# Re-searched queue orders and engine choices in a one-core four-layer linear-attention kernel

## The chip, the cores and the metric

One Trainium2 chip (trn2), one core of it. The metric is the device time of one execution in microseconds (us), taken as the median of several runs. Most runs lie within 0.5 us of their kernel's median, so the comparisons below use several rounds in which both kernels run on the same chip. All runs named here are of the undisturbed ("fast") state, with a granted TensorE clock of 0.999 or 1.000 (one run of b_head2, its slowest, has 0.996). The profiler's span of a run is about 2.1 us shorter than its device time (377.4 against 379.55 us for the run of the kernel before that was profiled).

Engines are called by the profile's names: PE (TensorE, matmuls), PEld (its weight loads), DVE (VectorE), ACT (ScalarE), POOL (GpSimd), SP (SyncE, here only the queue that issues transfers). An eviction is an operation of ACT or DVE that copies a matmul result out of PSUM (the tiles `ps`, which all 2519 matmuls of the trace of before write) to SBUF, where the program keeps the other operands. A transfer lands when its last part has arrived.

## The reference

Sequence 2048, width 512, 32 heads of 16, hidden width 1376, bf16. Two kinds of layer in turn, four in all:

```python
x = x + attn(layernorm(x));  x = x + glu(layernorm(x))     # layers L0/A0 and L1/B1
x = x + attn(layernorm(x));  x = x + glu(layernorm(x))     # layers L2/A2 and L3/B3

def attn(x):                                  # linear attention
    q, k, v = split_heads(x @ wqkv)
    phi = lambda z: concat(softmax(z @ w_phi), softmax(-(z @ w_phi)))   # per head, 16 -> 32
    kv, z = phi(k)^T v, sum_s phi(k)
    return (phi(q) kv) / (phi(q) z + 1e-6) @ wo
def glu(x):
    g = x @ W_gate
    return (g * (g > 0) * (x @ W_up)) @ W_down
```

In the kernel a row tile has 128 rows, so there are 16 tiles. "Key scaling" is the division of the exponentials of a key tile by their sums (phik), "query scaling" the same for queries (phiq), "numerator" is phi(q) kv (num). Before phi(q) can be multiplied it is transposed by a DMA transfer (qtr); there are 143 such 128 KB transposes in all.

## The kernel before

The program is a list of 3963 operations, each with an engine, what it reads and writes, and a name. Two tables decide how it runs: `ORDER` gives each engine's queue, as operation numbers in base 36, and `CHOICE` names the operations whose engine differs from the default. Waits are semaphores worked out from the tables.

```python
ORDER = {"act": ("29 26 6 25 ..."), "dve": (...), "pool": (...), "pe": (...), "sp": (...)}   # cut
for _e, _n in (("pool", ("kvf zero;...")), ("dve", (...)), ("act", (...))):                 # cut
    ...
            CHOICE[_x] = _e

def schedule(self):
    self._derive_deps()
    ops, TO = self.ops, self.TO
    seq = {e: [int(x, 36) for x in ORDER[e].split()] for e in ENG_NAMES}
    assert sorted(i for s in seq.values() for i in s) == list(range(len(ops)))
    ...                                                                                     # cut
```

The softmax here doesn't subtract the row's maximum and nothing guards it: scores larger than these inputs give would overflow.

Of the kernel before, what the change touches and what calls it, by code (L numbers as in the profile page):

```python
# [14 lines left out]
        "29 26 6 25 27 28 2a 2b 4t 2c 39 49 3u 4y 4e 44 5i 5n 58 5s 4j 6j 6k 67 73 72 8l 6d 84 6a 4o 83 8k 91 9x 9y 7r 96 9z c4 c5 9b c6 9g d9 da db b4 f9 f8 "  # L15
        "fm fl ay ee ef b2 eg gz gy fz h0 hx hw fy ij g5 g4 ik gb ga gg gh ii hv mk mj n4 n3 mu mt lm lq lt ne nd nn no nt r8 o5 o4 rf of op oq jv kn p0 pa pb "
        "vg pl pw pv vk q6 qg qh qr s1 ko sd sc sn xw xt sx sy t8 lg tt tj ti zn u4 ue u3 zu up uo uz wd wo wp x9 wz xa m8 ru ym yn xk z7 11o z8 yx 10k 11s zi "
        "10l 11v 10v 142 w2 12t yb 149 146 134 13p 135 13f 109 159 14z 13q 15a 15u 12a 15v 15k 14o 16x 178 177 17i 1b7 16m 18l 1aw 1c9 1db 1ad 1by 1d0 1e6 1dv "
        "1ea 1f0 1fg 1ew 1em 1gj 1fw 1gk 1fc 1gi 1jm 1hk 1hl 1hj 1kb 1fs 1ib 1ic 1kr 1l7 1g8 1ia 1j2 1j3 1gx 1ll 1lk 1j1 1m9 1ma 1nv 1k6 1ob 1mz 1my 1lj 1or "
        "1l3 1kn 1p7 1nn 1m8 1mn 1no 1mx 1pl 1pk 1ly 1q9 1nm 1o7 1nc 1qa 1pj 1qz 1qy 1on 1rq 1rp 1q8 1s4 1p3 1qx 1s3 1py 1ro 1t5 1t6 1s5 1s6 1t8 1qn 1t7 1u7 "  # L20
        "1ua 1u8 1xr 1uw 1uv 1u9 1xx 1y3 1uy 1ym 1yn 1ux 1z1 1z2 1y9 1yl 1zh 1zg 1z0 1zv 1zw 1zf 24t 1zu 24u 255 24v 24w 256 258 230 257 25u 25t 25h 25i 25k "
        "25w 25v 25j 26q 271 27d 272 22j 27n 27c 27z 27o 27y 289 28a 28l 28k 28v 28w 297 29h 296 29i 29t 29s 2be 23c 23x 2bp 2bq 24i 2cc 2cb 2c1 26f 2c0 2dj "
        "2cn 2cm 2di 2dt 2b3 2e5 2du 2e4 2ef 2eg 2er 2eq 2ft 2fu 2hu 2i5 2i6 2ih 2ig 2j2 2ir 2j3 2a7 2is 2d7 2kg 2k6 2kh 2k5 2l2 2l3 2ks 2kr 2mh 2le 2mg 2ld "
        "2fi 2hb 2ju 2m5 2qa 2pz 2qb 2n8 2ql 2qw 2qx 2qm 2sa 2r7 2sl 2sb 2r8 2ny 2sw 2sx 2t7 2sm 2pg 2t8 2um 2tj 2ti 2ul 2g8 2rz 2mv 2ua 2vw 2x5 2ak 2v0 2xg "
        "2xr 2xh 2od 2y3 2xs 2y2 2vd 2yd 2yp 2ye 2yo 2z0 2zb 2yz 2zm 2za 2zl 2gl 2wo 2zw 2zx 308 2wb 307 30z 2oq 31c 30m 322 "),
    "dve": (
        "2z 30 33 3a 3b 3e 3l 3m 3v 3k 3w 3p 2m 53 3z 5d 5x 5z 5t 5v 5u 60 5y 5w 7i 7g 7f 7h 6l 64 6m ao 74 ap 75 an am 85 7t 86 8m a0 7x 8n 7v a3 a1 a4 c7 ca "
        "c8 cb dc df b0 fa dg fn dd fo fb eh ek el ei em h1 h2 fq h4 hy hz h5 i1 il im i0 in io j2 j1 j3 j4 ix jd iz je iy j0 k6 jj k7 ku ky l1 l2 jo l3 l4 jp "
        "l6 l7 lv lw ju kc ly lz nu kh rc rg ki rh og ld ri o6 le or p1 rk pc pm rl vn vo q7 m5 px vq qi m6 xp qs kp s2 vs so se r4 sz xy xz t9 rr tk tu y1 u5 "
        "uf uq zr 13s we lh v0 zw zx zy zz rs vc 13t vz x0 wq w0 y8 y9 xb yo xl 13v 106 107 17w yy 15x zj 15y m9 z9 17x 15z 10m 17y 1b9 1ba 19o 10w 12u 11y 181 "  # L30
        "19p 14c 120 121 136 118 14d 13g 16c 14e 16d 150 19r 1cb 127 11k 13r 15b w3 128 1cc 18b 18c 15w 15l 1cd 14l 14m 16y 16j 16k 17j 179 17v 18i 18j 1a3 1a4 "
        "1bo 1bp 19b 1cq 1cr 18z 1aa 1ab 1b8 1dl 1ax 1dm 19n 1bv 1cx 1bw 1cy 1ca 1e8 1ds 1dt 1e7 1eb 1dc 1ey 1fe 1f3 1fh 1d1 1en 1ex 1jk 1kp 1fu 1fx 1gl 1fj "
        "1ft 12b 1k9 1fd 1l8 1ks 1gy 1dw 1hm 1g9 1hn 1j4 1j5 1gm 1id 1ha 1go 1nt 1l5 1nw 1mb 1ie 1i1 1hp 1mc 1la 1o9 1is 1k7 1jj 1p5 1oc 1gn 1os 1op 1ko 1p8 "
        "1lm 1ln 1n0 1ig 1n1 1n2 1l4 1lo 1pm 1lz 1lp 1nd 1np 1mo 1j7 1nq 1pn 1po 1r0 1pp 1r1 1o8 1r3 1qb 1qc 1s7 1s8 1oo 1p4 1rr 1rs 1se 1sf 1pz 1qo 1t9 1tg "
        "1rf 1xp 1ta 1th 1qe 201 1xs 1sw 1xv 202 203 20f 1xu 1ty 1tl 204 20g 1y1 208 209 1yo 1um 1y7 1y6 1yp 1z3 1ya 1yq 1z4 1yc 1zi 1zj 1zl 1zx 1zy 200 1zz "
        "20a 21r 21q 21s 21p 20d 221 222 227 22u 22v 22c 23n 23o 22d 20m 22i 248 249 235 236 265 23b 20n 2et 26r 266 2gm 2eu 24f 23u 23v 273 2ev 27e 2gn 280 "
        "28b 27p 2at 24g 2au 28m 2go 2lg 298 2cx 29j 28x 29u 2cy 2j5 26c 2j6 26d 2n9 2na 2f8 2f9 2bf 23d 2a6 2lh 2br 2aj 2li 2ll 2b0 2h1 2cd 2c2 2h2 2d4 2ff "
        "2co 23y 2b1 2or 2os 2dk 2nc 2d5 2fg 2e6 2eh 2dv 2es 2tl 2fv 2jk 2jl 2g7 2ra 2ou 2b4 2hv 2rb 2i7 2ow 2lv 2tm 2lw 2gk 2it 2h8 2h9 2ii 2j4 2no 2m2 2k7 "
        "2np 2rf 2m3 2jr 2js 2l4 2ki 2kt 2p6 2p7 2lf 2mi 2mu 2rp 2nv 2nw 2rq 2n7 2m6 2u0 2u1 2qc 2q0 2hc 2jv 2op 2oc 2vm 2pd 2qn 2qy 2pe 2r9 2sc 2rw 2rx 2vn "
        "2t9 2sn 2sy 2tk 2un 2uz 2u7 2u8 2vt 2vu 2vc 2x6 2xt 2ub 2xi 2wa 2yf 2wn 2y4 2yq 2s0 2zn 2z1 2zy 2zc 309 30l 30y 31b 31o 320 "),  # L40
    "pool": (
        "2p 0 1 4 2t 5 2w 2x 31 2 2u 2n 2o 32 3c 34 3d 3n 3o 2y 3x 3y 3f 2s 2r 2q 2v 61 62 66 63 69 6c 3 7j 7l 7k 7m 7n 7o 6n 7p 7q 76 ar aq as au at 87 av aw "
        "ax 8o a2 a5 c9 cc dh fp fc de fd ff ej h3 fs en h6 l5 lu lx rj jw vp jx vr vt xx kq y0 zv y2 100 13u 13x 17z li 11w rv 160 11x 14a 14b ma 162 19q 1bb "
        "1be 11z 10a yc 19t 14f 1bc yd 1cg rw w4 1ce 10b 18m 14p 1ec 16n 1ed 1f1 1f2 1fi 1fy 1fz 1jn 1kc 1kd 1bz 18n 16o 1ke 14q 1jo 1kt 1jp 1c0 1ku 1l9 1ae "
        "1ho 12c 1nx 1p9 1dx 1pa 1if 1od 1md 1ny 1oe 1ot 1j6 1d2 1ou 1me 1n3 1af 1r2 1nr 1ns 1sg 1sj 1s9 1sc 1rt 1qd 1sa 1tb 1te 1tc 1xt 206 1sh 1ti 1tj 20h "
        "1y4 1y5 20k 1xy 1xz 1y0 1ru 1yr 1yb 1z6 1z5 1zk 20i 20b 20o 20r 20p 2ew 2gr 2gp 22k 22l 2ey 2j7 2j8 23e 26g 2ja 24j 2nb 24k 23z 2lj 2ot 2b5 2tn 2to "
        "2tq 2d8 26h 2ne 2rc 2rd 2d9 2hd 2fj 2fk 2nz 2o0 2jw 2vx 2ph 2m7 2s1 2pi 2uc 2vy "),
    "pe": (
        "7 8 9 a b c d e f g h i j k 4p 4q 4r 4s l m n o p q r s t u v w x y z 35 36 37 38 10 11 12 13 14 15 16 17 3g 3h 3i 3j 18 45 46 47 48 3q 3r 3s 3t 4z 50 "
        "51 52 59 5a 5b 5c 4u 4v 4w 4x 4a 4b 4c 4d 40 41 42 43 5e 5f 5g 5h 4f 4g 4h 4i 5j 5k 5l 5m 19 1a 1b 54 55 56 57 1c 1d 1e 5o 5p 5q 5r 1f 1g 6f 6g 6h 6i "  # L50
        "1h 6y 6z 70 71 1i 1j 1k 1l 1m 1n 1o 8g 8h 8i 8j 1p 1q 1r 1s 6p 1t 1u 7z 80 81 82 1v 1w 6o 1x 1y 1z 20 21 22 23 24 4k 4l 4m 4n 9l 9m 9n 9o 8x 8y 8z 90 "
        "9h 9i 9j 9k 9p 9q 9r 9s 9t 9u 9v 9w 6q 6r 6s 6t 77 78 79 7a 92 93 94 95 bo bp bq br bs bt bu bv 6u 6v 6w 6x 97 98 99 9a 88 89 8a 8b bw bx by bz c0 c1 "
        "c2 c3 ct cu cv cw 9c 9d 9e 9f cx cy cz d0 d1 d2 d3 d4 d5 d6 d7 d8 f4 f5 f6 f7 fh fi fj fk 7b 7c 7d 7e 8c 8d 8e 8f 8p 8q 8r 8s dy dz e0 e1 a6 a7 a8 a9 "
        "e6 e7 e8 e9 e2 e3 e4 e5 ea eb ec ed fu fv fw fx ae af ag ah cd ce cf cg cl cm cn co 8t 8u 8v 8w aa ab ac ad gm gn go gp gi gj gk gl ai aj ak al ch ci "
        "cj ck gq gr gs gt gu gv gw gx di dj dk dl g0 g1 g2 g3 hn ho hp hq dq dr ds dt ia ib ic id cp cq cr cs dm dn do dp hr hs ht hu g6 g7 g8 g9 du dv dw dx "
        "es et eu ev eo ep eq er gc gd ge gf ie if ig ih mb mc md me mf mg mh mi f0 f1 f2 f3 ew ex ey ez h7 h8 h9 ha hf hg hh hi i2 i3 i4 i5 ip iq ir is hb hc "
        "hd he hj hk hl hm i6 i7 i8 i9 it iu iv iw j5 j6 j7 j8 j9 ja jb jc mz n0 n1 n2 mv mw mx my k2 k3 k4 k5 jf jg jh ji jy jz k0 k1 ml mm mn mo mp mq mr ms "
# [55 lines left out]
    "sp": (  # L113
        "2d 2e 2g 2f 2h 2i 2j 2k 2l 68 65 6e 6b 7u 7s 7y 7w b5 b1 az bg b3 bi bm b7 bn bb fg fe bk b9 ft fr bc ba b6 bd b8 be bj bf bh l8 bl m0 nv lf rm m7 s3 "
        "vu y3 101 w1 ya rt 108 13w wf 13y 161 122 12v 163 182 16e 14g 180 1bd 19s 18d 14n 1cf 19u 1bf 16l 129 18k 1ch 1a5 1bq 1cs 1dn 1ac 1bx 1e9 1cz 1du 1ez "
        "1ff 1kq 1ay 1fv 1jl 1ka 1l6 1k8 1p6 1nu 1oa 1oq 1xq 1sk 1tf 1xw 1y2 1sb 1sd 1y8 1tk 1tm 1si 207 205 1td 20c 20e 20l 23p 20j 24a 20s 267 26s 23w 20q "
        "24h 2av 2ex 2gq 2gs 2ez 2cz 2bg 2fa 2lm 2jb 26e 2fh 2d6 2b2 2h3 2j9 2lk 2ox 2jm 2lx 2hw 2nd 2nf 2ov 2nq 2ha 2m4 2jt 2tr 2p8 2re 2rg 2nx 2rr 2tp 2pf "
        "2q1 2vo 2u2 2ry 2u9 2vv 2x7 321 "),
}
# [257 lines left out]
CHOICE = {}  # L377
# [836 lines left out]
```

## Time and profile before

| | kernel before |
|---|---|
| device time, median of the first 3 runs | 379.65 us (379.38 to 380.29) |
| profiled span | 377.4 us |
| busy PE / DVE / ACT / POOL | 367.7 / 276.2 / 227.0 / 130.8 us |
| idle time of PE between its first and last matmul (worked out in the prediction) | about 8.7 us |

The prediction shows the page, the chain, the waits and the windows of this kernel. The view of the timeline: start in us, busy time in us, engine, line of the kernel, operation, output and inputs with their shapes, how many; a bracket gives the idle time before it and what ended it. First, the root of tile 3 on POOL (9.43), the scaling of tile 3 on DVE (10.33), and what POOL runs beside it:

```profile
9.43 0.86 POOL L631 TENSOR_TENSOR rstd<-rv,mhalf 128x1 f32<-128x1 f32 x1
...
10.33 0.41 DVE L670 TENSOR_SCALAR ytile<-x_sb,mv,rstd 128x512 bf16<-128x512 bf16 x1
10.38 0.40 POOL L668 TENSOR_SCALAR nrx<-rstd 128x1 f32<-128x1 f32 x1
10.55 1.89 POOL L568 MEMSET vsb<- 128x128 bf16 x3
```

DVE starts 0.05 us before POOL's next operation.

### The profile page before, as it was taken

What the parts mean: (1) busy time and instruction counts of PE and PEld (TensorE: products, weight loads), DVE (VectorE), ACT (ScalarE), POOL (GpSimd) and SP (SyncE); (2) the same over time, 40 slices, a digit from 0 to 9 for tenths busy, and PEclk for the clock granted to TensorE, in tenths of its full rate; (3) what the DMA queues carried; (4) which work ended last, traced back from release to release, by engine and by line L of the source; (5) the groups of instructions that cost most, each with busy time, mean ns of one, the idle gap of its engine ahead of it and who ended that gap; (6) DMA issues with size and microseconds to landing.
All of it is one profiled execution on the core that took longest, in us unless ns stands there. A gap on an engine that the chain in (4) does not pass through costs nothing.

```text
span 377.4 us, 6882 instructions
## 1 busy us (share of the span) xinstructions
PE 367.7 (97%) x2519; PEld 203.9 (54%) x2565; DVE 276.2 (73%) x607; ACT 227.0 (60%) x463; POOL 130.8 (35%) x234
## 2 busy tenths in 40 slices
PE   6999999999999999999999999999999999999997
PEld 5654555877744454454444446577664454445443
DVE  5999998989968676459799999898984654342323
ACT  3999878765744127874677568584635451653450
POOL 6799941133344001350463577023221201000020
PEclk9999999999999999999999999999999999999999
DMA  7632794313326444310300045335543442142012
GB/s 233 173 76 52 187 240 149 77 33 56 78 43 94 97 64 84 70 30 14 70 2 1 2 81 95 79 63 95 83 83 75 81 86 56 28 71 70 30 42 70
DMA packets 87856, 29.33 MB, mean 78 GB/s; under 512 B 79792, under 2 KB 86800, under 8 KB 87824
## 3 DMA queue, kind: packets, MB, share of 16 engines
q1 hardware_dynamic: 84368, 25.86, 33.7%
q10 hardware_dynamic: 3456, 3.05, 2.5%
q8 instruction: 20, 0.33, 0.4%
q14 instruction: 12, 0.10, 0.1%
HBM read 7.91 MB, written 2.10 MB: 27 GB/s over the span
## 4 chain that ended last, share of the span: by engine, by line
PE 85%; POOL 7%; DVE 3%; issue 2%; ACT 1%; DMA 1%; POOLq 0%; DVEq 0%
PE ps L962 37%; PE ps L1011 20%; PE ps L725 7%; PE ps L942 7%; POOL expk L750 5%; PE ps L822 5%; PE ps L988 3%; PE ps L921 2%; PE ps L787 1%; PE ps L886 1%; DMA hT<-in_A_wqkv_dram 1%; DVE Zk L744 1%; POOL rstd L648 1%; PE ps L868 1%; PE ps L539 0%
## 5 line engine op out<-in xcount | busy, mean ns | idle before, releaser
L962 PE MATMUL ps<-yT,Wgu 128*128 128x512 bf16 (+2 forms) x870 | 150.8, 320 | 0.6
L962 PEld LDWEIGHTS ps<-yT,Wgu 128*128 128x128 bf16 x880 | 78.5, 98 | 58.8 <-ACT expk L970 1.0
L964 ACT ACTIVATE gate_sb<-ps 128x512 bf16<-128x512 f32 (+2 forms) x110 | 50.7, 480 | 55.1 <-PE ps L962 41.8
L1011 PE MATMUL ps<-Wd,hT 128*128 128x512 bf16 (+4 forms) x354 | 79.3, 373 | 0.5
L1011 PEld LDWEIGHTS ps<-Wd,hT 128*128 128x128 bf16 (+1 forms) x363 | 34.6, 98 | 39.5 <-DVE hT L972 0.7
L972 DVE TENSOR_TENSOR hT<-gate_sb,expk 128x512 bf16<-128x512 bf16 (+2 forms) x70 | 23.9, 361 | 30.4 <-ACT expk L970 21.4
L970 ACT ACTIVATE expk<-ps 128x512 bf16<-128x512 f32 (+2 forms) x70 | 32.0, 475 | 22.2 <-PE ps L962 19.5
L710 ACT ACTIVATE sq<-x_sb,nmr 128x512 bf16<-128x512 bf16 x48 | 34.6, 721 | 10.3 <-DVE x_sb L687 6.6
L744 DVE TENSOR_REDUCE Zk<-expk 128x64 f32<-128x1024 bf16 x32 | 38.1, 1203 | 1.0 <-ACT expk L737 0.7
L714 POOL TENSOR_TENSOR rstd<-rv,mone 128x1 f32<-128x1 f32 x32 | 18.6, 589 | 50.2 <-DVE rv L712 50.0
L1013 DVE SCALAR_TENSOR_TENSOR x_sb<-ps,rstd,x_sb 128x512 bf16<-128x512 f32 (+2 forms) x33 | 23.9, 728 | 16.1 <-PE ps L1011 13.5
L942 PE MATMUL ps<-wo_p,oT 128*128 128x512 bf16 x118 | 30.8, 379 | 0.6 <-DVE oT L413 0.3
L975 DVE TENSOR_TENSOR hT<-gate_sb,ps 128x512 bf16<-128x512 bf16 (+2 forms) x40 | 21.7, 544 | 12.6 <-ACT gate_sb L964 6.4
L855 POOL TENSOR_TENSOR expq<-expq,rho 128x256 bf16<-128x256 bf16 x36 | 22.2, 624 | 24.4 <-DVE rho L852 23.7
L847 DVE TENSOR_REDUCE Zq<-expq 128x64 f32<-128x1024 bf16 x24 | 28.8, 1204 | 0.8 <-POOL rho L852 0.5
L687 DVE SCALAR_TENSOR_TENSOR x_sb<-ps,x_sb 128x512 bf16<-128x512 f32 x32 | 21.9, 687 | 8.6 <-PE ps L942 7.8
L750 POOL TENSOR_TENSOR expk<-expk,rZk 128x1024 bf16<-128x1024 bf16 x13 | 25.9, 2005 | 0.6 <-DVE rZk L746 0.6
L755 POOL TENSOR_TENSOR expk<-expk,rZk 128x512 bf16<-128x512 bf16 x17 | 19.1, 1134 | 11.8 <-DVE rZk L746 11.5
L822 PE MATMUL ps<-Wqp,yT 128*128 128x512 bf16 x91 | 22.8, 379 | 0.3
L725 PE MATMUL ps<-Wkp,yT 128*128 128x512 bf16 x84 | 22.0, 379 | 0.2
L725 PE MATMUL ps<-wv_p,yT 128*128 128x512 bf16 x85 | 21.9, 379 | 0.2
L712 POOL TENSOR_SCALAR rv<-rv 128x1 f32<-128x1 f32 x22 | 4.3, 203 | 45.3 <-ACT sq L710 45.3
(126 smaller groups left out, 514.1 us busy)
## 6 DMA issues: line engine op xcount, KB each, us to landing
out_dram<-x_sb ACTq DMA_DIRECT2D x15, 128.0 KB, 1.7
x_sb<-in_A_x_dram SPq DMA_DIRECT2D x3, 512.0 KB, 5.0
Wgu<-in_B_W_up_dram SPq DMA_DIRECT2D x4, 344.0 KB, 5.5
Wgu<-in_B_W_gate_dram SPq DMA_DIRECT2D x4, 344.0 KB, 4.3
Wd<-in_B_W_down_dram SPq DMA_DIRECT2D x5, 256.0 KB, 3.3
yT<-ytile SPq DMA_TRANSPOSE x56, 2.5
qT<-expq SPq DMA_TRANSPOSE x40, 2.5
x_sb<-in_A_x_dram SPq DMA_DIRECT2D x4, 128.0 KB, 3.6
```

The lines of the kernel that those rows point to most:

```text
L710: op("act", lambda e: e.activation(k.sq[:], k.x_sb[:, t, :], ACT.Square, scale=-float(D), bias=k.nmr[:, t, :], accum_out=k.rv1[:, t, :]), ...
L725: op("pe", (lambda ic, bank, W: lambda e: e.matmul(k.pb[bank][:], k.yT[:, ic, t * 128:(t + 1) * 128], W[:, ic, :], start=(ic == 0), stop=( ...
L744: op("dve", lambda e: e.tensor_reduce(k.Zk[:, zb, :], k.expk[:, t, :, :, :].rearrange("p g s (h f) -> p (g s h) f", f=16), AX.X, ALU.add), ...
L750: op("pool", lambda e: e.tensor_tensor(kv, kv, k.rZk[:, rb, :].unsqueeze(2).to_broadcast([P, 64, 16]), ALU.mult), [r("expk", t, 0), r("exp ...
L822: op("pe", (lambda ic, bank, tt: lambda e: e.matmul(k.pb[bank][:], k.yT[:, ic, tt * 128:(tt + 1) * 128], k.Wqp[:, ic, :], start=(ic == 0), ...
L847: op("dve", lambda e: e.tensor_reduce(k.Zq[:, b, :], k.expq[:, t, :, :, :].rearrange("p g s (h f) -> p (g s h) f", f=16), AX.X, ALU.add), ...
L942: op("pe", (lambda c, bank: lambda e: e.matmul(k.pb[bank][:], k.oT[:, ob, c, :], k.wo_p[:, c, :], start=(c == 0), stop=(c == NC - 1)))(c, ...
L962: op("pe", (lambda bank, W, ic, fc, Mf: lambda e: e.matmul(k.pb[bank][0:Mf, 0:n], W[:, ic, fc * 128:fc * 128 + Mf], k.yT[:, ic, c0:c0 + n] ...
L964: op("act", (lambda Mf, gb, gs: lambda e: e.activation(k.gate_sb[0:Mf, gs, 0:n], k.pb[gb][0:Mf, 0:n], ACT.Relu))(Mf, gb, gs), [self.RP[gb] ...
L970: op("act", (lambda Mf, ub, up: lambda e: e.activation(up[0:Mf, 0:n], k.pb[ub][0:Mf, 0:n], ACT.Copy))(Mf, ub, up), [self.RP[ub]], ru, 170 ...
L972: op("dve", (lambda Mf, up, gs, u: lambda e: e.tensor_tensor(k.hT[0:Mf, u, 0:n], k.gate_sb[0:Mf, gs, 0:n], up[0:Mf, 0:n], ALU.mult))(Mf, u ...
L1011: op("pe", (lambda fc, Kf, u, c0, bank, m0, m1: lambda e: e.matmul(k.pb[bank][:, m0:m1], k.hT[0:Kf, u, c0:c0 + 128], k.Wd[0:Kf, fc, m0:m1] ...
```

## The change

A scheduler searched the orders and engines once more. The issues of the initial loads keep their order; the early layer-norm scalings may now take POOL (none does); the table load is modelled as 250 instead of 1450 ns, which is a number for the scheduler only. No arithmetic, tile or transfer is added or removed. The new tables put 106 operations on another engine (56 from POOL to DVE, 40 from DVE to POOL, 5 each way between ACT and DVE) and reorder the rest.

```diff
 ORDER = {
     "act": (
-        "29 26 6 25 27 28 2a 2b 4t 2c 39 49 3u 4y ...          # all five queues replaced, cut
+        "29 26 6 25 27 28 2a 2b 39 2c 3k 49 5d 4y ...
@@ CHOICE: the three lists of names replaced, cut
-        op("act", lambda e: e.activation(k.sq[:, 0:1], ones_c[:, 0:1], ACT.Exp), ..., 1450, "table")
+        op("act", lambda e: e.activation(k.sq[:, 0:1], ones_c[:, 0:1], ACT.Exp), ..., 250, "table")
-            self.op2("act" if on_act else "dve", apply, dep, dst, {"dve": 407, "act": 825}, f"{tag} apply {t}", 250.0)
+            how = CHOICE.get(f"{tag} apply {t}", "act" if on_act else "dve")
+            other = "act" if how == "dve" else "pool" if t < 9 and how == "act" else "dve" if how == "act" else "act"
+            dd = {"dve": 407, "act": 825, "pool": 2090}
+            self.op2(how, apply, dep, dst, {e: dd[e] for e in (how, other)}, f"{tag} apply {t}", 250.0)
```

The numbers of `ORDER` say nothing to a reader. These are three stretches of it, with the operations' names:

```text
POOL, start      before: rv1 3 | rstd 3 | nrx 1 | v ones 3 | v ones 2 | v ones 1 | h10t zero | rv1 4
                 after:  nrx 1 | rv1 3 | rstd 3 | mask4 | h10t zero | v ones 2 | rv1 4
POOL, 224-235 us before: phiq 6 1 | ... | phik 11 1 | phik 12 1 | rx 15 | phik 13 1 | phik 13 0 | phik 14 0 | phiq 6 0 | phiq 5 0
                 after:  phiq 3 1 | ... | phiq 6 0 | ... | phik 11 1 | rx 15 | phik 13 0 | phik 12 1 | phik 13 1 | phik 14 0
SP, 228-244 us   before: qtr 3 0 | qtr 3 1 | qtr 1 0 | qtr 4 1 | qtr 4 0 | qtr 2 0 | qtr 5 0 | qtr 5 1 | qtr 6 1 | otr 2
                 after:  qtr 3 0 | qtr 6 0 | qtr 4 0 | qtr 5 1 | qtr 4 1 | qtr 3 1 | otr 2
```

## The prediction

> **What bounds the kernel now.** I read the page's busy shares first, then the chain that ended last in order of time, then the waits of the weight loads, then the windows by stage. The first view says which engine is full.
>
> ```profile
> span 377.4 us, 6882 instructions
> ...
> PE 367.7 (97%) x2519; PEld 203.9 (54%) x2565; DVE 276.2 (73%) x607; ACT 227.0 (60%) x463; POOL 130.8 (35%) x234
> ...
> PE 85%; POOL 7%; DVE 3%; issue 2%; ACT 1%; DMA 1%; POOLq 0%; DVEq 0%
> ```
>
> PE is busy nearly always and carries 85% of the chain. Busy PE is not PE at its peak, so I need its floor. The chain in order of time gives the pace of each matmul width, since there matmuls stand back to back:
>
> ```profile
> 9.72 0.45 PE ps L585 x8
> 120.13 5.18 PE ps L962 x24
> 133.95 0.99 PE ps L988 x12
> 227.60 0.76 PE ps L787 x24
> 248.84 2.18 PE ps L962 x20
> ...
> 370.68 3.70 PE ps L1011 x19
> ```
>
> So 128 columns take 56 ns, 512 take 216, 192 take 82.5, 68 take 32, 256 take 109; the 144-wide ones stand at about 63 (0.25 us for 4). Counts from the loops of the code: 1333 of 512 columns (128 each of v, k, q, wo; 480 gate/up; 341 down) make 287.9 us; 240 of 256: 26.2; 11 of 384 at some 162: 1.8; 128 of 192: 10.6; 64 of 144: 4.0; 267 of 128: 15.0; 448 of 68: 14.3; four small ones 0.4. That is 360.2 us of real matmuls. Another 70 are dummies that multiply ones by ones: 3.9 us. Sum 364.1. The first matmul starts at 1.6 us, the last ends at 374.4; the 3.0 us after it are residual and store. So 374.4 - 1.6 - 364.1 = about **8.7 us is all the idle time PE has**. Where it lies is in the waits of the weight loads, taken stretch by stretch (0 to 14 us, 50 to 68, 230 to 252, 252 to the end):
>
> ```profile
> PEld ps L539 <- POOL ones L527: 1.6, 1, 1.6
> PEld ps L678 <- DVE ytile L670: 1.4, 1, 1.4
> PEld ps L585 <- DMA hT<-in_A_wqkv_dram: 0.8, 1, 0.8
> ...
> PEld ps L921 <- issue: 0.8, 2, 0.5
> PEld ps L886 <- DVE expk L413: 0.7, 1, 0.7
> ...
> PEld ps L942 <- DVE oT L413: 0.4, 1, 0.4
> ...
> PEld ps L962 <- ACT expk L970: 1.0, 3, 0.3
> PEld ps L1011 <- DVE hT L972: 0.7, 2, 0.4
> ```
>
> Added up, these views give 4.5 us before 14 us (1.6 of it the lead-in already taken off), 1.1 from 14 to 50, 2.1 from 50 to 68, 1.9 from 68 to 230, 1.8 from 230 to 252, 2.1 after. They over-count a little (11.9 against 8.7), as each counts a weight load's normal spacing too. The windows show which other engines are full meanwhile:
>
> ```profile
> 14.00:53.00 39.00, 38.68 (x306) 20.52 (x311) 38.51 (x55) 37.35 (x57) 35.76 (x42) 1.00 0.54 108
> 53.00:66.00 13.00, 11.81 (x98) 6.61 (x96) 11.16 (x30) 8.99 (x13) 1.50 (x3) 1.00 0.58 201
> 66.00:120.00 54.00, 53.58 (x468) 36.39 (x476) 47.24 (x125) 32.43 (x95) 16.28 (x34) 1.00 0.33 63
> 120.00:230.00 110.00, 109.36 (x593) 52.42 (x604) 85.14 (x173) 67.28 (x131) 42.34 (x76) 1.00 0.26 49
> ```
>
> From 14 to 53 us PE, DVE, ACT and POOL are all at 92% or more: nobody can take work from anybody. From 66 us on PE alone is full, with the clock at 1.00.
>
> [...] 624 against 468 ns for the 128x256 scaling, 1152 against 428 ns for the 128x512 sum; and only operations between SBUF tiles trade places with POOL in the diff, PSUM evictions only between ACT and DVE.
>
> **The change part by part.** No matmul, tile, transfer or arithmetic is added or removed. Of 3963 operations 106 change engine; the rest are reordered within their queues.
>
> *Layer-norm scaling on GpSimd.* The code now lets the early scalings take POOL, but comparing the engine lists none of them does. Worth 0. Likewise the new 250 ns for the table load is only a number for the scheduler.
>
> *Engine moves.* POOL to DVE, 56: 17 query scalings (468 ns on DVE, 624 on POOL, from the rows by form), 4 key scalings (827, 1134), 2 sums (428, 1152), 5 denominators' products (222, 335), 1 (268, 445), 7 ratios (179, 308), 13 variance fixes (145, 203), 7 negations (140, 274). DVE gains 17.6 us, POOL loses 26.3. DVE to POOL, 40: 6 query and 5 key scalings, 2 sums, 6 small products (2, 3 and 1 of three kinds; the second 184, 272), 5 ratios, 12 variance fixes, 4 negations: DVE loses 12.3, POOL gains 18.8. ACT and DVE swap ten PSUM evictions, DVE +0.35, ACT nearly 0. Net: DVE 276.2 + 5.7 = **about 282**, POOL 130.8 - 7.5 = **about 123**. All of it lies beside PE. By the time at which these operations stood before, DVE gets some 1.7 us more between 60 and 100 us, 1.1 from 100 to 120 and 1.3 from 240 to 260, almost nothing before 60.
>
> *Start, 0 to 14 us.* Five more dummies (43 instead of 38) run before the fourth transpose of the key weights, in time that waits for input anyway; so five fewer stand later: 5 x 56 = 0.28 us at best. The copy of transposed tile 1 goes to ACT and that of weight block 0 to DVE. The second weight transpose stands ahead of tile 2's, which takes 4 x 56 = 0.22 us off what follows the arrival of tile 2, so the second v eviction on ACT could go at some 11.1 us instead of 11.29. These overlap; I take -0.3 us. More is not to be had: the inputs' issues are fixed, and tile 2 arrives when it arrives.
>
> *14 to 53 us.* Same work on four full engines, the POOL chain of key scalings (1.93 us each) in the same order: the 0.2 us carries through, nothing adds.
>
> *53 to 66 us.* I compared the queues: key/value mask, first denominators, num 0, q 11, q 10, num 1, output transpose, the two last feature-major q groups, num 2 stand in the same order on PE, with two pairs swapped that wait for the same eviction. The 2.1 us of waits stay. 0.
>
> *66 us to the end.* PE has about 5 us of small waits by the over-counting view, some 3.5 in truth. At 230 to 252 the order (num 0, q 10, q 9, otr 0, num 1, wo 0, num 2) is the same, so 1.2 us of these stay. Of the remaining 2.3 a new search may save a few tenths and a fuller DVE may cost a few: -0.1.
>
> Sum: -0.3 + 0 + 0 - 0.1 = -0.4 us: **379.2 us**.
>
> **The rivals.** First, the search finds real gains in the small waits: half of the late 2.3, plus 0.5 at the start, plus some of 50 to 68 us: -2.2, so 377.4. For it: the waits are of 0.2 to 0.7 us, which order alone could fix. Against: the orders around the largest are unchanged. Second, DVE becomes the bound from 60 to 120 us, where it has only about 7 us of idle time and gets 2.8 more; PE has PSUM banks to free there. Each late eviction would cost 0.2 to 0.4 us; a handful makes +1.5, so 381. For it: 47.2 of 54 us is an average and some slices are full. Against: the moved operations are mostly off the eviction path. Third, the late weights: the DMA share from 50 to 60 us is 1.02, and the order of the 18 weight loads and of the query transposes among them changes. If an output-projection block or the last gate block lands late, PE waits at 60 or 66 us: +1, so 380.6. Against: before, DMA falls to 0.08 at 60 us, 5 us ahead of the first gate matmul, and the new order puts the projection blocks earlier.
>
> **Range and chances.** The rivals sit at -2.2 and +1.5; runs of one kernel spread over 0.9 us. 377.7 to 380.9 should hold 8 in 10. Faster by 2% needs 7.6 us out of 8.7 us of idle time, half of it before the inputs land: 1 in 100. Slower by 2% needs a broken stage: 2 in 100. Within 2%: 97 in 100.
>
> **What would show it.** PE busy should be within 1 us of 367.7; DVE 280 to 284 and POOL 121 to 126 show the engine moves. The key scaling chain on POOL should start 0.1 to 0.3 us earlier than 18.46 us. The 0.7 us wait on the feature-major numerator's eviction and the 0.4 us on the output transpose's copy should still be there. I am wrong if waits of the weight loads from 66 us on fall below 2 us or exceed 8, if the first gate matmul waits for DMA, or if the stage before 53 us moves by more than 0.5 us.

The sum came to -0.4 us, so 379.2 us. The 216 ns for 512 columns in the count rest on the 24 matmuls in 5.18 us of the chain shown; that no pace can be lower, which would make 364 us a floor, is not shown. The 0.2 to 0.4 us for a late eviction are an estimate; single waits of weight loads for evictions late in the trace of before are as long (0.2 for `ACT vsb`, 0.3 for `ACT expk`, 0.4 for `DVE oT`).

## More of the kernel before

A fill is a memset.

The operations that the argument touches. The layer-norm scaling of tiles 2 and 3 of the first layer ("L0 apply") waits for POOL's reciprocal root ("L0 rstd") and feeds PE's transposes:

```python
op("pool", lambda e: e.tensor_tensor(k.rstd[:, t0:t1, :], k.rv1[:, t0:t1, :], k.mhalf[:, 0:n], ALU.pow), ...)   # "L0 rstd t"
op("dve", lambda e: e.tensor_scalar(k.ytile[:, yb, :], k.x_sb[:, t, :], k.mv[:, t, 0:1], k.rstd[:, t, :],
                                    op0=ALU.subtract, op1=ALU.mult), ...)                                       # "L0 apply t"
```

Fills on POOL that may run at any time before their first use:

```python
for st in range(NSLAB):
    op("pool", ... e.memset(k.vsb[:, st*4:st*4+4, :, 16:17], 1.0) ...)          # "v ones st"
op("pool", lambda e: e.memset(k.h10t[:], 0.0), ...)                             # "h10t zero"
op("pool", lambda e: e.tensor_tensor(k.mask4[:], k.mask8[:, 0:4], k.mask8[:, 4:8], ALU.add), ...)   # "mask4"
op("pool", lambda e: e.tensor_copy(k.kvf[:, :, 136:144], ...), ...)             # "kv ones"
```

Key scaling in two halves u, by choice on DVE or POOL; query scaling and the two transposes of a query tile:

```python
self.op2(..., e.tensor_tensor(kv, kv, k.rZk[...].to_broadcast([P, 32, 16]), ALU.mult), ...)     # "A2 phik t u"
for u in range(2):
    self.op2("pool", ... e.tensor_tensor(ev, ev, k.rho[...].to_broadcast([P, 4, 4, 16]), ALU.mult) ...)   # "A2 phiq t u"
    self.dma_tr(... e.dma_start_transpose(qb[:, u*4:u*4+4, :], k.expq[:, t, u*4:u*4+4, :, :]...) ...)     # "A2 qtr t u", SP
```

Second, near the end of the keys of the last attention, POOL's key scalings 13 0 and 14 0 (in one group) and DVE's 14 1:

```profile
231.39 2.69 POOL L755 TENSOR_TENSOR expk<-expk,rZk 128x512 bf16<-128x512 bf16 x2
...
232.47 0.69 DVE L755 TENSOR_TENSOR expk<-expk,rZk 128x512 bf16<-128x512 bf16 x1
```

## The result, and the profile after

The changed kernel takes **381.44 us** (median of 4 runs, 381.28 to 381.97) where the kernel before took 379.56 (median of 4) beside it: ratio 1.0048, 95% interval 1.0031 to 1.0066. A ratio here is the mean time of one kernel's fast runs over the mean of the other's in the same rounds, so it is not quite the quotient of the medians. Where a difference in us is given with a ratio below, it is the ratio less 1, times 379.5: here 1.8 us. The time lies inside the 2% band, but 2.2 us over the predicted time and just outside the predicted range.

The page of the changed kernel, its span, busy times and chain by engine, against 377.4 us, 276.2 for DVE, 130.8 for POOL and 85% PE before:

```profile
span 379.3 us, 6884 instructions
...
PE 368.9 (97%) x2520; PEld 204.3 (54%) x2565; DVE 281.2 (74%) x623; ACT 226.4 (60%) x463; POOL 124.0 (33%) x218
...
PE 87%; DVE 5%; DMA 2%; ACT 2%; issue 1%; POOL 1%; SPq 1%; ACTq 0%
```

The engine moves came out as worked out (DVE about 282, POOL about 123). The windows by stage, two of those that the prediction read (columns: window, its length, busy us of PE, PEld, DVE, ACT and POOL with counts, clock, DMA share, GB/s):

```profile
66.00:120.00 54.00, 53.45 (x468) 36.36 (x476) 48.50 (x130) 31.10 (x92) 18.54 (x37) 1.00 0.34 66
120.00:230.00 110.00, 109.20 (x584) 52.34 (x594) 85.95 (x177) 67.10 (x132) 37.45 (x67) 1.00 0.24 48
```

DVE is fuller from 66 to 230 us by 2.1 us (48.50 + 85.95 against 47.24 + 85.14), and PE's busy time there is the same to 0.3 us. To see where the time went I took the starts of PE's weight loads in both traces, added up the matmul work (dummies left out), and read the time at which each kernel had the same amount done:

| matmul work done, us | before, at us | after, at us | difference |
|---|---|---|---|
| 2 | 9.78 | 9.22 | -0.56 |
| 6 | 14.59 | 15.10 | +0.51 |
| 50 | 62.56 | 63.01 | +0.45 |
| 222 | 235.72 | 236.11 | +0.39 |
| 226 | 240.31 | 241.09 | +0.78 |
| 230 | 244.51 | 246.37 | +1.87 |
| 358 | 372.57 | 374.46 | +1.89 |

So the 1.9 us arise in three places and nowhere else: about **1 us between the first transposes and 15 us** (a lead of 0.56 becomes a lag of 0.5), **0.4 us near 238 us**, and **1.1 us near 244 us**. From 15 to 235 us, where DVE is fuller, nothing is lost. The waits of the weight loads confirm it (window 0 to 14 us, then 230 to 252; columns: waiting line, what it waited for, us in total, times, longest):

```profile
PEld ps L682 <- DVE ytile L674: 1.2, 1, 1.2
```
```profile
PEld ps L925 <- DMA qT<-expq: 1.1, 1, 1.1
PEld ps L925 <- issue: 0.5, 1, 0.5
PEld ps L946 <- DVE oT L414: 0.4, 1, 0.4
```

The first line looks like the 1.4 us of before, but is another wait. Before, PE waited for tile 2, whose input came late. Here PE waits for tile 3, and the timeline shows why: its scaling on DVE, of 0.41 us before, takes 1.31:

```profile
9.63 0.57 POOL L632 TENSOR_TENSOR rstd<-rv,mhalf 128x1 f32<-128x1 f32 x1
10.17 0.20 POOL L573 TENSOR_TENSOR mask<-mask 128x4 bf16<-128x4 bf16 x1
10.23 1.31 DVE L674 TENSOR_SCALAR ytile<-x_sb,mv,rstd 128x512 bf16<-128x512 bf16 x1 [0.39 <-POOL rstd L632]
10.30 0.52 POOL L572 MEMSET h10t<- 128x512 bf16 x1
10.76 0.64 POOL L569 MEMSET vsb<- 128x128 bf16 x1
```

Now POOL's next operation starts 0.06 us *before* DVE's, and DVE ends at 11.54, 0.14 us after the last of POOL's three. I call this the hold. What makes it in the hardware no trace here shows. The hold itself stands in the trace of before too, though I had not asked it: of 21 half key scalings on DVE, the 11 that started while POOL was free took 0.68 to 0.69 us, and of the 10 that started beside a running POOL operation 9 ended 0.54 to 0.55 us after it, whenever they had started (in the tenth it was POOL that was held: its rho 2, recorded 0.05 us ahead of DVE, took 0.78 us against 0.25 for most others of its kind; so recorded starts this close do not by themselves tell which of the two is held). The sum reductions (Zk) took 1.2 us in either case.

The second place shows the same hold. DVE's key scaling 14 1 now starts 0.08 us after POOL's 13 1 (the last but one of the group of three) and takes 1.52 us instead of 0.69:

```profile
231.49 3.53 POOL L759 TENSOR_TENSOR expk<-expk,rZk 128x512 bf16<-128x512 bf16 x3
...
232.58 1.52 DVE L759 TENSOR_TENSOR expk<-expk,rZk 128x512 bf16<-128x512 bf16 x1
```

The third place is a transfer. The chain of waits in order of time (start, us, what):

```profile
239.98 1.27 SPq L862
...
241.29 4.34 DMA qT<-expq
```

Half 1 of query tile 3 is transposed by the sixth issue of its stretch, at 241.29 us instead of 230.13, although its data had been ready at 225.6 us. Being late was not enough to hurt: the median landing is 2.5 us after the issue, so 243.8, and PE came to it at 244.5. But this one took 4.34 us. In the view of the DMA, for the stretch from 243 to 244 us, one packet does not belong to the transposes:

```profile
q8 instruction: 1, 0.02, 7.5%
```

(columns: queue and kind, packets, MB, share of the 16 engines' time). The profile counts it as instructions; I call it a fetch. It holds 16 KB: the 20 packets of queue 8 hold 0.33 MB. Both traces together hold 21 transposes issued 0.9 to 2.3 us before such a packet of queue 8; 18 of them took over 3.7 us to land. Of the other 265, 7 did, 5 of these at 43 to 52 us beside the weight loads. (I chose the window of 0.9 to 2.3 us after seeing the data. The twelve traces of the experiments below, which had no part in that choice, give 115 of 129 in the window and 38 of 1587 outside it.) This can be read in the kernel before too: its packet at 242.5 us simply meets no transpose in flight (one had landed at 242.14 us, the next was issued at 243.11).

### The profile page after: what moved, and what is told of

Read it like the earlier page. It is cut to its first block, busy times and chain, and to the rows that moved or that the text cites. A ratio compares the mean times of both kernels' runs of the same rounds, so it can differ in the third digit from the quotient of the medians.

```text
span 379.3 us, 6884 instructions
## 1 busy us (share of the span) xinstructions
PE 368.9 (97%) x2520; PEld 204.3 (54%) x2565; DVE 281.2 (74%) x623; ACT 226.4 (60%) x463; POOL 124.0 (33%) x218
## 4 chain that ended last, share of the span: by engine, by line
PE 87%; DVE 5%; DMA 2%; ACT 2%; issue 1%; POOL 1%; SPq 1%; ACTq 0%
PE ps L966 36%; PE ps L1015 20%; PE ps L729 7%; PE ps L946 7%; PE ps L770 5%; PE ps L826 4%; PE ps L992 3%; PE ps L872 2%; PE ps L925 1%; PE ps L791 1%; DMA x_sb<-in_A_x_dram 1%; DMA qT<-expq 1%; PE ps L890 1%; DVE stats L624 1%; ACT expk L741 1%
## 5 line engine op out<-in xcount | busy, mean ns | idle before, releaser
L1015 PE MATMUL ps<-Wd,hT 128*128 128x512 bf16 (+3 forms) x357 | 79.4, 373 | 0.3
L759 POOL TENSOR_TENSOR expk<-expk,rZk 128x512 bf16<-128x512 bf16 x18 | 20.9, 1175 | 18.2 <-DVE rZk L750 16.1
L859 POOL TENSOR_TENSOR expq<-expq,rho 128x256 bf16<-128x256 bf16 x25 | 15.6, 628 | 27.3 <-DVE rho L856 21.1
L729 PE MATMUL ps<-wv_p,yT 128*128 128x512 bf16 x86 | 22.7, 384 | 0.2 <-issue 0.2
L716 POOL TENSOR_SCALAR rv<-rv 128x1 f32<-128x1 f32 x21 | 5.3, 256 | 43.2 <-ACT sq L714 43.1
```

The source lines that it names most:

```text
L729: op("pe", (lambda ic, bank, W: lambda e: e.matmul(k.pb[bank][:], k.yT[:, ic, t * 128:(t + 1) * 128], W[:, ic, :], start=(ic == 0), stop=( ...
L1015: op("pe", (lambda fc, Kf, u, c0, bank, m0, m1: lambda e: e.matmul(k.pb[bank][:, m0:m1], k.hT[0:Kf, u, c0:c0 + 128], k.Wd[0:Kf, fc, m0:m1] ...
```

## The experiments

**Theory.** The loss is three accidents of order: (1) POOL's operations straight behind the root of tile 3 start 0.06 us before DVE's scaling, which is held until the last of them is done; (2) the same near 232 us, plus a query scaling ahead of the first denominators; (3) one transpose late enough to meet an instruction fetch. **Rival.** The 106 engine moves cost: a fuller DVE holds PE up. All kernels gave right results. All were timed in five rounds (b_eng has four runs, a_tail six), in three groups that each shared the runs of the kernel before: groups 1, 2 and 3 with medians of before of 379.54, 379.28 and 379.62 us (rows 1 to 4, 5 to 8 and 9 to 12 of the table). Compare by the ratio and not by the medians across groups.

The edits are moves within the queues, applied after `ORDER` is read. This is the whole mechanism; each experiment below shows only its `MOVES`:

```diff
     seq = {e: [int(x, 36) for x in ORDER[e].split()] for e in ENG_NAMES}
+    at = {}
+    for o in ops:
+        at.setdefault(o.name, o.idx)
+    for name, e, side, anchor in MOVES:
+        for q in seq.values():
+            if at[name] in q:
+                q.remove(at[name])
+        seq[e].insert(seq[e].index(at[anchor]) + (side == "after"), at[name])
```

| run | what | us, median | ratio to before, 95% interval |
|---|---|---|---|
| a_sp | changed, transpose early | 380.62 | 1.0030 (1.0018 to 1.0042) |
| a_head | changed, fills away | 380.57 | 1.0031 (1.0019 to 1.0043) |
| a_tail | changed, 230 us stretch mended | 380.76 | 1.0037 (1.0023 to 1.0050) |
| a_all | changed, all three | 379.30 | 0.9997 (0.9985 to 1.0009) |
| b_sp2 | before, transpose late | 380.86 | 1.0041 (1.0028 to 1.0053) |
| b_sp3 | before, transpose one place less late | 379.52 | 1.0009 (0.9996 to 1.0021) |
| b_head | before, fills behind the root | 380.38 | 1.0029 (1.0017 to 1.0042) |
| best | a_all and PE's waits filled | 379.85 | 1.0013 (0.9999 to 1.0027) |
| b_head2 | b_head with nrx 1 put ahead | 381.72 | 1.0064 (1.0051 to 1.0078) |
| a_head1 | changed, one fill away | 381.05 | 1.0037 (1.0024 to 1.0049) |
| b_eng | before, with the 106 engine moves | 383.98 | 1.0115 (1.0101 to 1.0129) |
| a_eng | changed, without the 106 engine moves | 382.03 | 1.0066 (1.0053 to 1.0078) |

### a_sp: the transpose early

```diff
+MOVES = [("A2 qtr 3 1", "sp", "after", "A2 qtr 3 0")]
```

> The changed kernel with one transpose, the one of query tile 3 half 1 in the last attention, moved in the transfer queue to directly behind its other half, ahead of four others. My theory (a late transfer makes 1.1 us of the loss): it is issued near 235 us instead of 241.3, lands before 240, the 1.1 us wait of the weight loads for it at 244.5 us goes, and the kernel takes 1.0 to 1.1 us less than the changed one (381.4 to about 380.4, +0.8 over the kernel before). Rival (the loss is spread, a fuller VectorE holds PE up everywhere): PE finds another wait there and the time stays within 0.3 us of 381.4. Second rival: the four transposes behind it come later and one of them is then waited for, so half of the gain is given back.

Measured: 380.62 us, 1.1 us over before instead of 1.8, so 0.7 gained. The transpose is issued at 235.19, lands at 237.74, and no weight load waits for a DMA at 242 to 248 us. By the count of matmul work its stretch gained 1.06 us against the changed kernel's trace; this profiled run had begun 0.2 us later at the first tiles. The four transposes put behind it were not waited for. The first theory holds for this part; the size at the end is below the expected 1.0 to 1.1.

### a_head: the three fills away

```diff
+MOVES = [("kv ones", "pool", "after", "A0 phik 13 0"), ("mask4", "pool", "after", "A0 phik 13 0"),
+         ("h10t zero", "pool", "after", "mask4"), ("v ones 2", "pool", "before", "L0 rv1 2")]
```

> The changed kernel with the three GpSimd fills that stood straight behind the reciprocal root of tile 3 taken away from there: the ones of v go into an idle gap at 7 us, the 4-column mask and the zeros of h10t (with the ones of the kvf columns, to make room) behind the last key scaling on GpSimd, at 52 us. Theory (VectorE's scaling of tile 3 stood still [...] until GpSimd paused): that scaling takes 0.4 us instead of 1.31, tile 3's transposes come 0.9 us earlier, the first key scaling on GpSimd starts 0.5 to 0.9 us before 18.96 us, and the time falls by 0.45 to 0.9 us to 380.5 to 381.0. Rival (the head is set by the arrival of the data and by other queues, the long scaling is slack): the scaling gets short, but the first key scaling starts within 0.1 us of 18.96 and the time stays within 0.2 us.

Measured: 380.57 us, as expected. The timeline of this kernel has the scaling back at its old length, though it starts no earlier:

```profile
10.27 0.41 DVE L688 TENSOR_SCALAR ytile<-x_sb,mv,rstd 128x512 bf16<-128x512 bf16 x1 [0.43 <-POOL rstd L646]
```

The first key scaling on POOL starts at 18.10 us: 0.86 before the changed kernel's 18.96, and 0.36 before the 18.46 of the kernel before. The rest of the start was thus better than before by what the prediction had said, and the hold had hidden it.

### a_tail: the stretch at 230 us

```diff
+MOVES = [("A2 phiq 6 0", "pool", "after", "A2 phik 14 0"), ("A2 phik 12 1", "pool", "before", "L2 rx 15"),
+         ("A2 phiq 5 0", "dve", "after", "A2 o 0")]
```

> The changed kernel with three moves near 230 us: the query scaling 6 0 on GpSimd behind the last key scaling and key scaling 12 1 ahead of the square root step of tile 15, so that GpSimd is through with key tile 13 before VectorE starts 14 1; and the query scaling 5 0 on VectorE behind the first output division. Theory (a collision [...] of 0.83 us, and an operation ahead of the first denominators): key scaling 14 1 takes 0.69 us instead of 1.52, the masks start 0.3 us earlier and the first denominator 0.7 us earlier, and PE's waits there shrink by 0.35 us. The end moves by only 0.0 to 0.4 us, since PE must wait for the late transpose behind it all the same: I expect -0.1. Rival (the collision is repaid elsewhere): the same small number, but the wait at 244.5 us does not grow; under my theory it grows from 1.1 to about 1.4.

Measured: six runs of 379.95, 379.95, 380.52, 380.99, 381.06 and 381.76 us, a wider spread than any other kernel here. The profiled run was one of the fast ones. In it key scaling 14 1 takes 0.80 us instead of 1.52, and 0.25 us are gained near 238 us. Another 1.1 us were gained at 244 us, which neither theory expected: the late transpose, issued at 240.59, landed in 2.47 us. The instruction packet came at 243.0, when it had just landed, 2.4 us after the issue; in the changed kernel it came 2.0 us after it. So a shift of some 0.4 us decides about 1.1 us. That the longer runs of this kernel met the fetch is what the spread suggests; only one was profiled, so it is not shown. Nor does a_tail, with three moves at once, tell the share of the hold from that of the query scaling ahead of the first denominators.

### a_all: all three

```diff
+MOVES = a_sp + a_head + a_tail
```

> All three edits together. Theory: the three causes make the whole loss of 1.9 us, so 381.4 - 1.1 - 0.45 to 0.9 - 0.35 = 379.1 to 379.5, equal to the kernel before or up to 0.5 us under it. Rival (engine moves themselves cost a part): it stays at 380.3 or above.

Measured: 379.30 us, level with before (interval -0.15% to +0.09%); the loss of 1.8 us is gone. DVE stays as full as in the changed kernel:

```profile
PE 368.4 (98%) x2520; PEld 204.2 (54%) x2565; DVE 280.3 (74%) x623; ACT 226.1 (60%) x463; POOL 124.4 (33%) x218
```

In this trace the fetch at 242.5 us hits another transpose (4 1, issued 240.46, landed after 4.2 us), which nobody waits for. This settles the rival for the changed kernel: its 106 engine moves, in its orders, cost nothing once the three places are mended. By the count of matmul work a_all is 0.4 us ahead of before at 15 us and 0.3 at 372, so nothing is lost in between either.

### b_sp2 and b_sp3: the transpose late in the kernel before

```diff
+MOVES = [("A2 qtr 3 1", "sp", "after", "A2 qtr 6 1")]      # b_sp2
+MOVES = [("A2 qtr 3 1", "sp", "after", "A2 qtr 5 1")]      # b_sp3
```

> The kernel before with its transpose of query tile 3 half 1 put off in the transfer queue from 230 us to directly behind that of 6 half 1, so that it is issued near 241 us, as in the changed kernel. In both traces a block of instructions is fetched [...]at 242.5 to 243.3 us, and transposes issued 1 to 2.2 us ahead of such a fetch land after 4.0 to 4.4 us instead of 2.45. Theory (late issue plus the collision with the fetch): it lands after 245, PE waits for it 1 to 1.6 us at 243.7 us, and the kernel takes 1.0 to 1.6 us more than before. Rival (late issue alone; the landing is 2.45 us): it lands at 243.4 and nothing is lost, within 0.2 us. Rival (the loss lies elsewhere and PE only waits there because it is early): nothing is lost at the end.

> The control for the one before: the same transpose put off one place less, directly behind that of 5 half 1, issued near 239.7 us, nearly 3 us ahead of the fetch. Theory (collision with the fetch): it lands in the usual 2.45 us at 242.1, PE does not wait for it, and the time stays within 0.25 us of before. Rival (every late place in the queue costs by itself): it loses most of what the other one loses, 0.8 us or more.

Measured: b_sp2 380.86 us (+1.6), b_sp3 379.52 us (+0.3, interval -0.2 to +0.8, so no loss is shown, though 0.3 is just over the expected 0.25). In b_sp2 the transpose is issued at 240.79 us, lands after 4.15, and PE waits for it; an instruction packet of queue 8 starts at 242.8 us, 2.0 after the issue. The waits of the weight loads at 242 to 248 us:

```profile
PEld ps L932 <- DMA qT<-expq: 1.2, 1, 1.2
```

In b_sp3 the same transpose, one place earlier and issued at 239.66, lands in 2.47 us. The one that takes its old place, 6 1, is hit instead (issued 240.97, the packet at 243.2, landed after 4.27 us). PE does not need 6 1 yet. So the late place alone was nearly free here, and the place that met the fetch cost 1.6 us in the one run in which PE needed the tile at once. (The 4.0 to 4.4 us of the expectation are too narrow: the 21 transposes above took 2.45 to 4.7 us.)

### b_head, b_head2 and a_head1: the fills, in the kernel before and one by one

```diff
+MOVES = [("mask4", "pool", "after", "L0 rstd 3"), ("h10t zero", "pool", "after", "mask4"),       # b_head
+         ("v ones 2", "pool", "after", "h10t zero")]
+MOVES = [("L0 nrx 1", "pool", "before", "L0 rv1 3")] + b_head                                    # b_head2
+MOVES = [("v ones 2", "pool", "before", "L0 rv1 2"), ("kv ones", "pool", "after", "A0 phik 13 0")]  # a_head1, in the changed kernel
```

> The kernel before with the 4-column mask, the zeros of h10t and one fill of ones put straight behind the reciprocal root of tile 3 on GpSimd, as they stand in the changed kernel; nothing else. Theory (VectorE's scaling of tile 3 [...] and GpSimd's queue does not let go between the three): that scaling takes 1.2 to 1.4 us instead of 0.41, tile 3's transposes on PE come some 0.9 us later, the first key scaling on GpSimd starts 0.5 to 0.9 us after 18.46 us, and the time grows by 0.5 to 0.9 us. Rival (in the changed kernel it is the different order of VectorE or the ACT queue that costs): the scaling stays at 0.4 us, or grows without moving the end, within 0.2 us.

> The earlier test of the fills in the kernel before had a second effect in it: the negated root of tile 1 stood behind the fills, and ScalarE's second v eviction waited 0.89 us for it. Here that small operation goes ahead of tile 3's reciprocal root, as in the changed kernel, and the three fills again follow that root. Theory [...]: the scaling of tile 3 still takes 1.2 to 1.4 us, no ScalarE eviction waits for GpSimd there, and the time grows by 0.4 to 0.9 us over before. Rival (the eviction was what cost): the scaling is long, but the time stays within 0.2 us of before.

> The changed kernel with only the last of the three fills (the ones of v) moved to the idle gap at 7 us; mask and zeros stay behind the reciprocal root. Theory ([...] each fill in a row adds its whole time): the scaling of tile 3 ends 0.15 us after the zeros do, so it takes 0.65 to 0.8 us instead of 1.31, and the kernel gains about 0.5 to 0.6 of the 0.87 us that taking all three away gave, so 380.9. Rival (it must wait for the first operation only, and something else made it long): 1.31 us stays, or it is 0.41 at once.

Measured: b_head 380.38 us (+1.1, over the expected 0.5 to 0.9). The scaling takes 1.31 us, the same as in the changed kernel, but a ScalarE eviction also waited 0.89 us for nrx 1 behind the fills, so the run does not separate the two; hence b_head2. That one cost more than expected, +2.4 us with 381.72, and the scaling took 2.40 us instead of 1.2 to 1.4:

```profile
10.49 2.40 DVE L684 TENSOR_SCALAR ytile<-x_sb,mv,rstd 128x512 bf16<-128x512 bf16 x1 [0.22 <-POOL rstd L645]
10.55 0.53 POOL L585 MEMSET h10t<- 128x512 bf16 x1
11.02 1.72 POOL L582 MEMSET vsb<- 128x128 bf16 x3
```

I had overlooked that without nrx 1 between them the kernel before's own two fills of ones follow at once. That DVE ends just after POOL's last fill held where my number failed: it ended at 12.89 us, 0.15 after the last of POOL's unbroken run (12.74). a_head1 tests it the other way, with one fill fewer, and hits in the scaling (0.73 us against 0.65 to 0.8). The time, 381.05 us against 380.9 expected, gained 0.4 us on the changed kernel instead of 0.5 to 0.6, which the noise doesn't tell apart:

```profile
10.09 0.73 DVE L686 TENSOR_SCALAR ytile<-x_sb,mv,rstd 128x512 bf16<-128x512 bf16 x1 [0.43 <-POOL rstd L644]
10.16 0.53 POOL L584 MEMSET h10t<- 128x512 bf16 x1
```

In all eight kernels whose scaling was long (changed, a_sp, a_tail, a_head1, b_head, b_head2, and b_eng and a_eng below) DVE ended 0.14 to 0.15 us after the *last* fill of an unbroken run of POOL, not after the operation that ran when DVE came. It was not so for the key scaling 14 1 of the changed kernel: it got in between two of POOL's (1.52 us, ended 0.55 us after the first of them, and POOL's next took 1.51 us instead of 1.06). Which property makes the difference is open. That b_head2 with no waiting eviction lost even more than b_head shows that the loss does not need the eviction. (The profiled run of b_head was the fastest of its five; by the count of matmul work it lost 0.4 us by 15 us and 0.6 at the end, less than the 1.1 of the mean.)

### b_eng and a_eng: engine moves without orders, orders without engine moves

Each of the 106 operations is put into the other engine's queue at the place that its start time in the trace of the starting kernel gives; two of the 106 lines:

```diff
+CHOICE["L0 ytrcopy 2"] = "dve"
+MOVES = [..., ("L0 ytrcopy 2", "dve", "before", "wtrcopy wk 1"), ...]
```

> The engine moves alone: the kernel before, with the 106 operations put on the engines of the changed kernel, each at the place in its new queue that its start time in the trace of before gives; all else keeps the order of before. VectorE should be busy some 281 us and GpSimd 124. Theory (a fuller VectorE lies beside PE and costs nothing; the loss came from order): within 0.4 us of before. Rival (the engine moves cost): 1 us or more over before.

> The orders alone: the changed kernel with the 106 operations put back on their engines of before, by their start times in the trace of the changed kernel. The fills behind the root of tile 3 and the late transpose are untouched by this. Theory: the scaling of tile 3 is long, the late transpose is waited for, and 1.3 to 2.0 us of loss stay over before. Rival (the engine moves cost): most of the loss goes, 0.7 us or less over before.

Measured: b_eng 383.98 us, +4.4 us where I expected 0.4 at most: a plain miss. a_eng 382.03 us, +2.5 us, more than the 1.3 to 2.0 expected. In b_eng, 1.5 us or more of it is the hold again. The copy of tile 2, moved to DVE, pushes its next copy to 9.79 us, so that DVE is busy when the root of tile 3 is done (9.96); POOL's nrx 1 then starts first (10.05 against 10.12), and five POOL operations pass:

```profile
10.12 2.41 DVE L892 TENSOR_SCALAR ytile<-x_sb,mv,rstd 128x512 bf16<-128x512 bf16 x1
10.23 1.73 POOL L790 MEMSET vsb<- 128x128 bf16 x3
...
11.56 0.83 POOL L793 MEMSET h10t<- 128x512 bf16 x1
```

DVE ends at 12.53, 0.14 us after the last of them. So the kernel before itself stood 0.05 us from this cliff. The other losses of b_eng, by the count of matmul work, are 0.9 us at 102 us, where PE waits 0.9 us for an eviction of numerator 9 that now stands behind two query operations on DVE, and 1.0 us near 228 us, which I did not follow to its end; together with the start these make 3.4 of the 4.4 us. DVE's busy time in b_eng is 279.7 us, less than the 281.2 of the changed kernel, which is 2.5 us faster. So DVE's busy time does not order these kernels; what stands ahead of what does, as far as the losses were followed. In a_eng the scaling of tile 3 is as long (1.31 us) as in the changed kernel, as expected; the transpose was not waited for, because it was issued at 242.46 and landed in 2.5 us; some 1.3 us more than in the changed kernel were lost between 74 and 238 us. Neither half of the change stands alone: the orders are made for the engines. These two runs do not say what DVE's load costs by itself; the differences between 15 and 235 us above and a_all do.

### best: filling PE's waits

```diff
+MOVES = a_all + [("A0 wo 0 c", "pe", "before", "A0 num 2 6") for c in 0..3]
+              + [("A2 q 11 c", "pe", "before", "A2 wo 0 0") for c in 0..3]
+              + [("A0 num 4 4", "pe", "before", "B1 gu 0 10 0"), ("A0 num 4 5", "pe", "before", "B1 gu 0 10 0")]
```

> The three mends together with three fillings of PE waits that both kernels have: the four output projections of tile 0 in the first attention between the two last groups of numerator 2 (a wait of 0.735 us for a PSUM bank at 58.5 us), the query projection of tile 11 ahead of the output projection of tile 0 in the last attention (waits of 0.45 and 0.39 us at 239.5 and 240.4 us), and two numerator products ahead of a gate group (0.33 us at 64.9 us). If the waits are idle time of PE alone, as my reading has it that PE's idle time is the only thing that counts, the time falls by 0.7 + 0.8 + 0.1 from 379.3 to about 377.7 us, 0.5% under the kernel before. Rival: what is moved ahead finds its own bank taken, or puts off the chain behind it, and half or all of it comes back: 378.5 to 379.5.

Measured: 379.85 us, no better than before. The rival was right in kind, and the time lies even above its 378.5 to 379.5. Where a_all waited 0.7 us at 58 to 61 us, this kernel waits twice 0.3. At 238 to 246 us the waits aimed at are gone and others stand in their place; the weight loads now wait for

```profile
PEld ps L729 <- DVE x_sb L719: 0.7, 1, 0.7
PEld ps L974 <- ACT expq L859: 0.5, 1, 0.5
```

where a_all waited 0.5, 0.4 and 0.3 us. My reading, which no run tests by itself, is that these PE waits are links of a chain (numerator, division, transpose, projection, residual, next layer norm): work put ahead of a link delays the link. No version tried beats the kernel before by more than the noise; a_all equals it.

## Why the prediction was wrong

- **Bound.** Right: PE bounds the kernel, the time changed only where PE's idle time did. PE busy came out 1.2 us up (368.9), just past the 1 us named.
- **Engine moves.** The busy times were right (281.2 and 124.0 against 282 and 123). That they lie beside PE was right in the changed orders: the difference between the kernels stays at +0.4 to +0.5 from 15 to 235 us. b_eng shows that this is no property of the moves. The two ratios of POOL to DVE are far apart: 624 to 468 ns is 1.3, 1152 to 428 is 2.7. And one reading of the costs was off without moving the sum: the mean of 827 ns for a key scaling on DVE mixes 0.68 us when free with up to 1.56 when held; the hold was hidden in this mean.
- **Start, "I take -0.3 us".** The step that failed first. The gains named in it came (-0.56 at the first matmuls; a_head's first key scaling 0.36 us ahead of before). What was missing is a term: POOL's queue behind the root of tile 3 had changed, and the hold turned that into 0.9 us. Measured +0.51 us at 15 us and +0.45 from there on in place of -0.3, and a first key scaling at 18.96 us, 0.5 later than before instead of 0.1 to 0.3 earlier. The prediction compared POOL with DVE by speed alone and did not look for holds, although 9 scalings held up for POOL could be seen in the trace of before. I also overlooked that both kernels carry a hold in their own timing model: in `schedule` a DVE operation with a `port` may start that long before the end of a POOL operation (250 of 407 ns for a layer-norm scaling, 135 of 683 for a key scaling, which leaves 157 and 548 ns after POOL's end, close to the 0.14 and 0.55 us measured). But there DVE waits only for the POOL operation placed just before it, and POOL's next waits for DVE: the model fits the scaling in between the mask and the zeros of h10t at its full speed, where the chip made it wait for the whole run.
- **14 to 53 us and 53 to 66 us, "carries through, nothing adds" and 0.** Right, and the waits of 0.7 and 0.4 us stayed as named.
- **66 us to the end, "At 230 to 252 the order is the same, so 1.2 us of these stay ... -0.1".** The step that failed most. I had compared PE's queue there, and not SP's and POOL's, which feed it. Measured +1.45 us: 0.35 to 0.4 near 238 us from the hold and the query scaling ahead of the first denominators (shares not separated; a_tail's trace won back 0.25), and 1.1 from the late transpose that met a fetch. From 252 us on the difference does not change at all.
- **Rivals.** The second came nearest in size (381) with the wrong cause (evictions at 60 to 120 us). The third looked at late transfers, but at weights at 50 to 66 us. The range failed because no rival priced a change of 1 us in a single queue position; in this kernel single positions were worth 0.9, 1.1 and 2 us.

By its sum: -0.3 became +0.45, and -0.1 became +1.45; together +1.9 us, as measured.

## What to carry to other kernels

When two schedules are compared, compare every queue that feeds the critical one, transfers and GpSimd included, and ask of each operation on DVE what POOL starts within 0.1 us of it. Here the layer-norm scaling took 0.41 us when it started 0.05 us ahead of POOL and 1.31 us when it started 0.06 us behind; a key scaling on DVE that was held ended 0.54 to 0.55 us after POOL's operation, the layer-norm scaling 0.14 to 0.15 us after the last of a whole run of fills. Keep fills that can run at any time away from places where POOL has just released DVE. A transfer like this one, with less than some 2 us to spare, is not safe (4.3 us to landing in place of 2.5): an instruction fetch may come between, and a harmless shift of a few tenths elsewhere decides whether it does.
